# Spectral transform and experts on one core: scatters untied from the early reads, first weights converted earlier, stage 1's table filled on the chip

## The chip, the cores and the metric

One core of a Trainium2 chip runs one program. The metric is device time in microseconds (us). Of the kernel before, three runs took 837.57 to 837.99 us, with a median of 837.95.

## What is computed

The reference is a chain of three pieces in fp32:

```python
X = np.fft.fft(np.fft.fft(x, axis=1), axis=2).real      # x: (8, 3072, 256)
x = X.reshape(24576, 256)                               # tokens
logits = x @ w_gate                                     # 8 experts
# each token goes to its best expert, in order of tokens, while the
# expert has room (capacity 768); tokens without room give zero rows
h = relu(disp[e] @ w1[e]);  y = h @ w2[e]               # 256 -> 1024 -> 256
out[token] = gate * y                                   # gate: softmax value of the expert
a, b = out @ mw1, out @ mw2                             # 256 -> 1024
result = ((a * b) @ w3) @ w_out                         # -> 24576 x 256
```

The eight experts have room for 6144 tokens, so with usual inputs they are full after the first two and a half of the eight batches of 3072 tokens. All other rows of the output are zeros.

## The kernel before, in words

**Batches and stages.** Only NSTAT = 3 batches are transformed and routed, the third in a reduced form ("half"). A transform is four stages. Batch b's x comes in four chunks j (`load`, L256, 768 KB each, the last chunk of batch 0 in two cuts). `fold` (L264) lets DVE add and subtract mirrored halves into the tile xf. `stage1` (L301) multiplies xf on TensorE by the table F: 20 blocks q of 96 x 104, of which chunk j uses blocks 4j to 4j+3, and chunk 0 also the special blocks 16 to 19. In blocks 1 to 15 only 2 of the 8 columns of each group are non-zero in a given row. ACT copies the result into T (L315). `stage_d` (L322) multiplies T by the tables R into z; `stage2` (L332) multiplies z by M into A and B, ACT copies B to Bs (L353 or L355), and DVE forms rows O = A -/+ Bs (L356, L357). `packs` (L193) cuts the 13 column groups of a batch into five packs, 1 + 3 + 3 + 3 + 3.

**Tables at the start.** `tables_a(j)` (L217) loads block group j of F, and with j = 0 the special blocks and the small table S. The program at L943 puts these loads on SP's queue between the chunks of x, then G and the gate weights W (`tables_b`), R and M (`tables_c`), I and X (`tables_d`). `warm` (L956) issues matmuls on zeros; `warm(4)` stands as eight matmuls in the trace. `setup_a` (L243) multiplies G by W for the gate, `setup_b` (L250) lets DVE put the products into R.

**Routing.** `route_a` (L408) and `route_b` (L471) find each token's expert and its rank there on DVE, and from them its slot, `sloti` (L502). Slots with a large value added (`over`, L501) fall out of bounds and are not written. Then POOL issues one indirect DMA for each group of up to 128 tokens (L509): it scatters rows of O (266 floats: the transformed row, the gate, the token's number) to the rows of the DRAM tensor `disp` that the slots name. There are 24 + 24 + 13 of them. `self.scat` lists the earlier scatters, and `declare_no_dep` says that a scatter needs to wait for none of those.

**Early rows.** The first 256 rows of experts 0 to 3 (`early`, L146) are expected to be filled by batch 0 alone. `seen` (L491) keeps how many tokens batch 0 gave each expert, at most 256; if any of these four falls short, the flag at the end makes a slower second part of the program run, which redoes everything. `hand_over` (L991) gives the memory of the x tiles to the experts' class `Mlp`, asks for the first four pieces of expert weights (`raw`, L565) and for the early rows (`load_rows`, L558, the tiles X). It runs in batch 1's part of the loop, before `route_b` issues batch 1's scatters. The scatters of batch 1 and of the half batch write `disp`, which the early reads read, so they wait until these reads are done.

**Order of the work.** All engines follow program order; on SP, TensorE, DVE and ACT it is written out by hand. The loop at L1003 works pack by pack: `todo` is a list of small jobs that `fill` takes from between the packs. In the half batch (`more` is false) `halves` are two jobs that `hand_over` made: `half` (L577) converts a piece of expert 0's w1 into a high part (ACT, `split` L159) and a low part (DVE, L160), w00h/w00l and w01h/w01l. They stand behind packs 4 and 5 (`i > 2`, L1019). Then `experts` (L696) runs: first the early rows (each expert's rows are transposed, L777, split into xh and xl, multiplied by w1 into ps_h, L163 to L165, passed through relu into hh and hl, L807 and L808, multiplied by w2 into ps_y), with the half batch's routing in between, then the rest. The rest's first rows need all scatters to be done (X, L562). Conversions of other weights and the clearing of the output (L188) run at times planned in `events`. At the end `products` (L854) computes the last piece.

Of the kernel before, what the change touches and what calls it, by code (L numbers as in the profile page):

```python
# [10 lines left out]
F32 = mybir.dt.float32  # L11
# [4 lines left out]
ALU = mybir.AluOpType  # L16
# [4 lines left out]
BIG = 1048576.0  # L21


def tables():
# [32 lines left out]
    for d0, d16, sg in ((F[0], F[16], 1), (F[17], F[18], -1)):  # L57
        put(d0, 1, 2, y(32))
        put(d0, 3, 2, sg * yc(32))
        for r in (0, 1):  # L60
            put(d16, r, 4 + 2 * r, y(32 * r + 16))
            put(d16, 3 - r, 4 + 2 * r, sg * yc(32 * r + 16))
    F = F.reshape(20, 96, 104).transpose(1, 0, 2)
    S = np.zeros((24, 4, 2))
    S[:, 1, 0] = 1
    S[:, 3, 0] = -1
    S[:, :2, 1] = 1
    S[:, 2:, 1] = -1
    S = S.reshape(96, 2)
    k2 = np.arange(128)  # L70
    M = np.zeros((2, 128, 128))
    for q in range(16):
# [53 lines left out]
def body(tc, cap, x, w_gate, w1, w2, mw1, mw2, w3t, w_out, cF, cS, cM, cR, cG, cI, cH, cT, out):  # L126
# [65 lines left out]
    class Transform:  # L192
        packs = [[0], [1, 2, 3], [4, 5, 6], [7, 8, 9], [10, 11, 12]]  # L193

        def __init__(self, stack, rows_stack, p_o, p_s):
            self.p_o, self.p_s = p_o, p_s
            self.scat, self.late, self.room = [], [], None
            self.kc = kc = pool("kc", 1, stack)
            self.p_T = pool("p_T", 2, stack)
            self.p_z = pool("p_z", 3, stack)  # L200
            self.p_b = pool("p_b", 2, stack)
            self.p_x = pool("p_x", 4, rows_stack, side="right")
            self.p_f = pool("p_f", 5, rows_stack, side="right")
            p_raw = pool("p_raw", 1, rows_stack, side="right")
            self.ps1 = pool("ps1", 3, stack, space=PSUM)
            self.psd = pool("psd", 3, stack, space=PSUM)
            self.psa = pool("psa", 2, stack, space=PSUM)
            self.F = kc.tile([96, 20, 104], F32, name="F")
            self.S = kc.tile([96, 2], F32, name="S")
            self.R = kc.tile([128, 414], F32, name="R")  # L210
            self.I = p_s.tile([128, 512], F32, tag="I", name="I")[:, :352]
            self.W = kc.tile([128, 2, 8], F32, name="W")
            self.M = kc.tile([128, 2, 128], F32, name="M")
            self.X = kc.tile([128, 4, 128], F32, name="X")
            self.G = p_raw.tile([128, 2, 256], F32, tag="raw", name="G")

        def tables_a(self, j):  # L217
            if j == 0:
                nc.sync.dma_start(out=self.F[:, 16:20], in_=cF[:, 16:20])
                nc.sync.dma_start(out=self.S, in_=cS)  # L220
            nc.sync.dma_start(out=self.F[:, 4 * j : 4 * j + 4], in_=cF[:, 4 * j : 4 * j + 4])

        def tables_half(self):
            self.H = self.p_s.tile([128, 283], F32, name="H")
# [76 lines left out]
        def stage1(self, T, xf, j):  # L301
            xf, mid = xf
            F = self.F

            def part(t):
                ps = self.ps1.tile([128, 4, 104], F32, tag="ps1", name="ps")
                for i in range(4):
                    if i or j:
                        nc.tensor.matmul(ps[:, i], xf[:, t, i], F[:, 4 * j + i], start=True, stop=True)
                        continue  # L310
                    nc.tensor.matmul(ps[:, 0], xf[:, t, 0], F[:, 17 if t else 0], start=True, stop=False)
                    if t:
                        nc.tensor.matmul(ps[0:1, 0], mid, F[:, 19], start=False, stop=False)
                    nc.tensor.matmul(ps[:, 0], xf[:, t, 4], F[:, 18 if t else 16], start=False, stop=True)
                nc.scalar.copy(  # L315
                    T[:, t, :, 32 * j : 32 * j + 32].rearrange("p k (i c) -> p i k c", c=8),
                    ps.rearrange("p i (k c) -> p i k c", c=8),
                )

            return [lambda: part(0), lambda: part(1)]  # L320
# [87 lines left out]
        def route_a(self, L, where, half):  # L408
# [37 lines left out]
                nc.vector.tensor_copy(meta[:, :, 1], tid)  # L446
            first_slot = self.narrow(n, "first_slot")
            nc.vector.tensor_scalar(first_slot, m, -float(CAPP), 8.0 * CAPP - 1.0, ALU.mult, ALU.add)
            return oh, pre, tot, first_slot, where, meta

        def route_m(self, r, half):
            where, meta = r[4:]
            jobs = []
            for o, k0, n in where:
                if half:
                    for (a, b), ps, js, ks in self.halves(k0, n):
                        nc.scalar.copy(o[ps, a:b, 8 + GATE : 8 + GATE + 2], meta[ps, js])
                    jobs += [(o, j, 8, k, 128 if 0 < k < 12 else 64) for j, k in enumerate(range(k0, k0 + n))]
                else:
                    nc.scalar.copy(o[:, :, 8 + GATE : 8 + GATE + 2], meta[:, k0 : k0 + n])  # L460
                    jobs += [(o, j, 8, k0 + j, 128) for j in range(n)]
                    a, b, gs = self.mates(k0, n)
                    if a < b:
                        nc.scalar.copy(o[:, a:b, 145 + GATE : 145 + GATE + 2], meta[:, gs])
                        jobs += [(o, j, 145, 24 - k0 - j, 128) for j in range(a, b)]
            return jobs
# [4 lines left out]
        def route_b(self, r, step, half):  # L471
# [27 lines left out]
            nc.vector.tensor_add(first_slot, first_slot, rank)  # L499
            over = self.narrow(n, "over")  # L500
            nc.vector.tensor_scalar(over, rank, float(cap), BIG, ALU.is_gt, ALU.mult)  # L501
            sloti = self.p_s.tile([128, 24], I32, name="sloti", bufs=2)  # L502
            if half:
                for _, ps, js, ks in self.halves(0, 13):
# [3 lines left out]
            for o, j, c, g, w in jobs:  # L508
# [7 lines left out]
                )  # L516
                for q in self.scat:
                    tc.declare_no_dep(i.ins, q.ins, reason="every token has a row of its own")
                self.scat.append(i)
            if not half:  # L520
                nc.vector.tensor_scalar_add(tid, tid, 3072.0)
# [28 lines left out]
    class Mlp:  # L550
# [7 lines left out]
        def load_rows(self, ch):  # L558
            e, c, nt = ch
            X = self.p_X.tile([128, CT, ROW], F32, name="X")  # L560
            r0 = e * CAPP + c * 128
            nc.sync.dma_start(out=X[:, :nt], in_=disp[r0 : r0 + nt * 128].rearrange("(t p) c -> p t c", p=128))  # L562
            return X

        def raw(self, kind, e, p):  # L565
# [374 lines left out]
            k = seq.pop(0)  # L940
            xq[k] = tr.load(*k, 2 if k == (0, 3) else 1)

    for j in range(4):  # L943
        if j == 3:
            tr.tables_b()
            tr.tables_a(j)
        prefetch(1)
        if j < 3:
            tr.tables_a(j)
    tr.tables_c()  # L950
    prefetch(1)
    tr.tables_d()
# [13 lines left out]
    def go(ops):  # L966
        for op in ops:
            op()
# [8 lines left out]
    D = nc.vector  # L977
    for j in range(4):
        ops, s1 = part(0, j, T, *([D] if j < 3 else [D, D]))
        go(ops + s1)  # L980
        if j < 3:
            warm(4)
        if j == 2:
            tr.setup_a()
        prefetch(1)
    tr.setup_b()
    if HALF:
# [3 lines left out]
    def hand_over():  # L991
# [5 lines left out]
        raws = [mlp.raw(*a) for a in parts]  # L997
        for ch in early:
            rows[ch] = mlp.load_rows(ch)
        mlp.raws = dict(zip(parts[2:], raws[2:]))  # L1000
        return [lambda a=a, r=r: mlp.half(*a, r) for a, r in list(zip(parts, raws))[:2]]

    for b in range(NSTAT):  # L1003
# [8 lines left out]
        for i in range(5):  # L1012
# [3 lines left out]
                s1.append(jobs)  # L1016
            if 1 <= i < 4:
                z.append(tr.stage_d(T, tr.packs[i + 1], fill))
            if not more and i > 2:  # L1019
                todo += halves[i - 3 : i - 2]  # L1020
            where += tr.stage2(L, tr.packs[i], z[i], half, fill)
        if not more:
            break
# [43 lines left out]
    if HALF or NSTAT < NBATCH:  # L1067
        v = nc.values_load(flagi[0:1, 0:1], min_val=0, max_val=FULL)
        with tc.If(v < FULL):
            with ExitStack() as st:  # L1070
# [2 lines left out]
                p_o = pool("p_o", 8, st)  # L1073
                with ExitStack() as fs:
                    tr = Transform(fs, fs, p_o, p_s)
                    for j in range(4):
                        tr.tables_a(j)
                    tr.tables_b()
                    tr.tables_c()
                    tr.tables_d()  # L1080
# [74 lines left out]
```

## Time and profile before

| what | before |
|---|---|
| median of three runs | 837.95 us |
| the profiled execution | 836.56 us |
| its span in the profile | 834.8 us |
| TensorE (PE) busy | 802.4 us, 96% |
| DVE, ACT, POOL busy | 453.9, 370.0, 149.6 us |
| mean granted TensorE clock | 0.981 |
| DMA moved | 94.65 MB |

The profile is one execution. Its span runs from the first to the last instruction; the execution is 1.8 us longer. PE is TensorE's matmuls, PEld its weight loads. Times in the rows are us from the span's start. "idle before <-releaser" is how long the engine stood still before an instruction, and what ended that.

### The profile page before, as it was taken

The page shows a single profiled execution, that of the slowest core. Times are in us where ns is not written, and L with a number is a line of the kernel's source. Part 1 is how long each engine was busy: PE and PEld are TensorE (multiplying, and loading weights), DVE is VectorE, ACT ScalarE, POOL GpSimd, SP SyncE. Part 2 cuts the span into 40 slices and gives each one's busy share as a digit, 9 for nine tenths or more (in the row PEclk, how much of TensorE's full clock was granted, in tenths as well). Part 3 has the DMA queues.
Part 4 walks back from the last instruction along what each step waited for, and adds up shares of the span by engine and source line. Part 5 has one row for each costly group of instructions (what it writes and reads, how often), then busy time and mean ns, then how long its engine had stood idle before and what let it go on. Part 6 is the DMA issues. An engine that isn't in the chain of part 4 may idle for free.

```text
span 834.8 us, 12890 instructions
## 1 busy us (share of the span) xinstructions
PE 802.4 (96%) x5032; PEld 738.0 (88%) x5032; DVE 453.9 (54%) x874; ACT 370.0 (44%) x756; POOL 149.6 (18%) x139
## 2 busy tenths in 40 slices
PE   9999899799999999999999999999999999999992
PEld 8788799699999999999979899898898998988981
DVE  5676675498878787898542523424225234242230
ACT  2555665265545454565443433424334234243230
POOL 0047588000000000000023112121131122111101
PEclk9999899799999999999999999999999999999996
DMA  9945698476849474877100000000000000000000
GB/s 237 259 132 182 200 316 273 125 220 239 260 147 279 147 245 149 259 219 259 66 1 20 7 27 13 13 26 2 25 20 6 26 14 14 26 7 20 25 10 22
DMA packets 68822, 94.65 MB, mean 113 GB/s; under 512 B 5036, under 2 KB 56280, under 8 KB 67696
## 3 DMA queue, kind: packets, MB, share of 16 engines
q1 hardware_dynamic: 63552, 80.90, 32.0%
q0 software_dynamic: 5200, 12.84, 4.3%
q8 instruction: 41, 0.67, 0.3%
q14 instruction: 29, 0.24, 0.1%
HBM read 55.72 MB, written 39.63 MB: 114 GB/s over the span
## 4 chain that ended last, share of the span: by engine, by line
PE 80%; issue 9%; DVE 4%; DMA 3%; POOL 2%; ACT 1%; POOLq 0%; ACTq 0%; DVEq 0%; SPq 0%
PE ps_h L164 5%; PE ps_h L163 5%; PE ps_y L164 5%; PE ps_h L165 5%; PE ps_y L165 5%; PE ps_y L163 5%; PE ps_a L164 4%; PE ps_b L165 4%; PE ps_a L165 4%; PE ps_b L164 4%; PE ps_b L163 4%; PE ps_a L163 4%; PE ps_o L898 4%; PE ps_o L897 4%; PE ps_o L896 4%
## 5 line engine op out<-in xcount | busy, mean ns | idle before, releaser
L884 DVE TENSOR_TENSOR g<-ps_b,sa 128x512 f32<-128x512 f32 x96 | 66.2, 690 | 185.8 <-PE ps_b L165 179.2
L159 ACT CAST gh<-g 128x512 fp32r<-128x512 f32 x96 | 59.6, 620 | 132.9 <-DVE g L884 131.8
L160 DVE TENSOR_TENSOR gl<-g,gh 128x512 fp32r<-128x512 f32 x96 | 76.8, 800 | 65.9 <-ACT gh L159 65.9
L807 ACT ACTIVATE hh<-ps_h 128x256 fp32r<-128x256 f32 (+1 forms) x160 | 67.8, 427 | 97.3 <-PE ps_h L165 92.3
L897 PE MATMUL ps_o<-wcl,gh 128*128 128x256 f32 x384 | 108.7, 283 | 0.0
L898 PE MATMUL ps_o<-wch,gl 128*128 128x256 f32 x384 | 108.7, 283 | 0.0
L896 PE MATMUL ps_o<-wch,gh 128*128 128x256 f32 x384 | 108.6, 283 | 0.0
L160 POOL TENSOR_TENSOR yl<-yt,yh 128x512 fp32r<-128x512 f32 x24 | 30.5, 1288 | 419.5 <-ACT yh L159 419.5
L808 DVE SCALAR_TENSOR_TENSOR hl<-ps_h,hh 128x256 fp32r<-128x256 f32 (+1 forms) x160 | 74.8, 472 | 33.7 <-ACT hh L807 33.3
L509 POOL DMA_INDIRECT disp<-O,sloti x61 | 71.4, 1171 | 75.2 <-DVE acc L523 49.1
L901 POOL DMA_INDIRECT out_dram<-o,toki x48 | 47.0, 979 | 175.2 <-ACT o L900 175.2
L163 PE MATMUL ps_a<-yh,wm0h 128*128 128x512 f32 x192 | 75.0, 390 | 1.0 <-ACT yh L159 1.0
L164 PE MATMUL ps_a<-yl,wm0h 128*128 128x512 f32 x192 | 75.0, 391 | 0.7 <-POOL yl L160 0.7
L164 PE MATMUL ps_b<-yl,wm1h 128*128 128x512 f32 x192 | 74.7, 389 | 0.0
L165 PE MATMUL ps_a<-yh,wm0l 128*128 128x512 f32 x192 | 74.7, 389 | 0.0
L163 PE MATMUL ps_b<-yh,wm1h 128*128 128x512 f32 x192 | 74.7, 389 | 0.0
L165 PE MATMUL ps_b<-yh,wm1l 128*128 128x512 f32 x192 | 74.7, 389 | 0.0
L896 PEld LDWEIGHTS ps_o<-wch,gh 128*128 128x128 f32 x384 | 73.7, 192 | 0.5
L897 PEld LDWEIGHTS ps_o<-wcl,gh 128*128 128x128 f32 x384 | 73.7, 192 | 0.5
L898 PEld LDWEIGHTS ps_o<-wch,gl 128*128 128x128 f32 x384 | 73.7, 192 | 0.0
L900 ACT ACTIVATE o<-ps_o,gate 128x256 f32<-128x256 f32 x48 | 22.8, 475 | 104.7 <-PE ps_o L898 104.7
L882 ACT COPY sa<-ps_a 128x512 f32<-128x512 f32 x96 | 56.3, 587 | 11.6 <-PE ps_a L165 11.4
(179 smaller groups left out, 1952.9 us busy)
## 6 DMA issues: line engine op xcount, KB each, us to landing
out_dram<-zer SPq DMA_DIRECT2D x48, 512.0 KB, 6.5
raw<-in_w_dram SPq DMA_DIRECT2D x44, 512.0 KB, 5.2
xr<-in_x_dram SPq DMA_DIRECT2D x11, 768.0 KB, 8.4
raw<-in_w3t_dram SPq DMA_DIRECT2D x16, 512.0 KB, 4.8
raw<-in_mw_dram SPq DMA_DIRECT2D x8, 512.0 KB, 4.3
X<-disp SPq DMA_DIRECT2D x12, 266.0 KB, 4.2
X<-disp SPq DMA_DIRECT2D x8, 399.0 KB, 6.0
raw<-in_w_out_dram SPq DMA_DIRECT2D x4, 512.0 KB, 4.7
```

The lines of the kernel that those rows point to most:

```text
L159: nc.scalar.copy(hi, src)
L160: eng.tensor_sub(lo, src, hi.bitcast(F32))
L163: nc.tensor.matmul(ps, wh, ah, start=first, stop=False)
L164: nc.tensor.matmul(ps, wh, al, start=False, stop=False)
L165: nc.tensor.matmul(ps, wl, ah, start=False, stop=last)
L509: i = nc.gpsimd.indirect_dma_start(out=disp[:, :], out_offset=bass.IndirectOffsetOnAxis(ap=sloti[0:w, g : g + 1], axis=0), in_=o[0:w, j, c ...
L807: nc.scalar.activation(hi, ps, AF.Relu)
L808: nc.vector.scalar_tensor_tensor(lo, ps, 0.0, hi.bitcast(F32), ALU.max, ALU.subtract)
L884: nc.vector.tensor_mul(g, b, sa)
L896: nc.tensor.matmul(ps, hi[:, ts], Wc[0][:, f], start=f == 0, stop=False)
L897: nc.tensor.matmul(ps, hi[:, ts], Wc[1][:, f], start=False, stop=False)
L898: nc.tensor.matmul(ps, lo[:, ts], Wc[0][:, f], start=False, stop=f == 7)
```

## The change

It has three parts. First, `tr.apart` collects the early reads, and scatters are declared independent of them; so that this holds in all cases, three DVE instructions in `route_b` push the slots of later batches' tokens that would fall into the early rows out of bounds. Second, the two jobs in `halves` stand one each behind packs 2 and 3 of the half batch instead of packs 4 and 5. Third, of F only the five special blocks are loaded (F0); for blocks 1 to 15 the non-zero columns alone are loaded (D, 26 for each block, with a pattern `own` and the table S behind them), and DVE multiplies them by the pattern into F1, in four instructions of 312 or 416 columns. The loads at the start are in another order: D, the first chunk of x, F0, the other three chunks, then the other tables. `warm(4)` becomes `warm(2)`, and `setup_a` moves from behind chunk 2 to the front of chunk 3's fold and stage 1.

```diff
@@ tables()
-    F = F.reshape(20, 96, 104).transpose(1, 0, 2)
+    D = np.stack([F[1:16, :, r, :, 2 * r : 2 * r + 2] for r in range(4)], 2)
+    D = D.reshape(15, 96, 26).transpose(1, 0, 2).reshape(96, 390)
+    own = np.broadcast_to(np.repeat(np.eye(4), 2, 1), (24, 4, 8)).reshape(96, 8)
+    F = F[[0, 16, 17, 18, 19]].reshape(5, 96, 104).transpose(1, 0, 2)
...
-    S = S.reshape(96, 2)
+    S = np.concatenate([D, own, S.reshape(96, 2)], 1)
@@ class Transform
-            self.F = kc.tile([96, 20, 104], F32, name="F")
-            self.S = kc.tile([96, 2], F32, name="S")
+            self.F0 = kc.tile([96, 5, 104], F32, name="F0")
+            self.F1 = kc.tile([96, 15, 104], F32, name="F1")
+            self.F = lambda q: self.F1[:, q - 1] if 0 < q < 16 else self.F0[:, max(0, q - 15)]
+            self.D = kc.tile([96, 400], F32, name="D")
+            self.S = self.D[:, 398:400]
...
-        def tables_a(self, j):
-            if j == 0:
-                nc.sync.dma_start(out=self.F[:, 16:20], in_=cF[:, 16:20])
-                nc.sync.dma_start(out=self.S, in_=cS)
-            nc.sync.dma_start(out=self.F[:, 4 * j : 4 * j + 4], in_=cF[:, 4 * j : 4 * j + 4])
+        def tables_a(self):
+            nc.sync.dma_start(out=self.F0, in_=cF)
+
+        def spread_a(self):
+            nc.sync.dma_start(out=self.D, in_=cS)
+            own = self.D[:, 390:398].rearrange("p (r t) -> p r t", t=2).unsqueeze(1)
+            for q0, n in ((0, 3), (3, 4), (7, 4), (11, 4)):
+                D = self.D[:, 26 * q0 : 26 * (q0 + n)].rearrange("p (k t) -> p k t", t=2).unsqueeze(2)
+                shape = [96, 13 * n, 4, 2]
+                nc.vector.tensor_mul(
+                    self.F1[:, q0 : q0 + n].rearrange("p q (k r t) -> p (q k) r t", r=4, t=2),
+                    D.to_broadcast(shape),
+                    own.to_broadcast(shape),
+                )
@@ route_b
+            if early and 0 < step < NBATCH:
+                held = self.narrow(n, "sm")
+                nc.vector.tensor_scalar(held, rank, float(need), BIG, ALU.is_le, ALU.mult)
+                nc.vector.scalar_tensor_tensor(held, r[6], 8.5 - len(early), held, ALU.is_gt, ALU.mult)
+                nc.vector.tensor_add(over, over, held)
...
                 for q in self.scat:
                     tc.declare_no_dep(i.ins, q.ins, reason="every token has a row of its own")
+                for q in self.apart:
+                    tc.declare_no_dep(i.ins, q.ins, reason="later batches put nothing into these rows")
@@ load_rows
-            nc.sync.dma_start(out=X[:, :nt], in_=disp[r0 : r0 + nt * 128].rearrange("(t p) c -> p t c", p=128))
+            self.asked = nc.sync.dma_start(
+                out=X[:, :nt], in_=disp[r0 : r0 + nt * 128].rearrange("(t p) c -> p t c", p=128)
+            )
@@ body
-    for j in range(4):
-        if j == 3:
-            tr.tables_b()
-            tr.tables_a(j)
-        prefetch(1)
-        if j < 3:
-            tr.tables_a(j)
+    tr.spread_a()
+    prefetch(1)
+    tr.tables_a()
+    prefetch(3)
+    tr.tables_b()
     tr.tables_c()
...
         ops, s1 = part(0, j, T, *([D] if j < 3 else [D, D]))
+        if j == 3:
+            tr.setup_a()
         go(ops + s1)
         if j < 3:
-            warm(4)
-        if j == 2:
-            tr.setup_a()
+            warm(2)
...
         for ch in early:
             rows[ch] = mlp.load_rows(ch)
+            tr.apart.append(mlp.asked)
...
-            if not more and i > 2:
-                todo += halves[i - 3 : i - 2]
+            if not more and 0 < i < 3:
+                todo += halves[i - 1 : i]
```

## Rows read from the trace of the kernel before

**Rows 1.** The page, parts 1 and 5 (name, busy us, count, mean ns, idle).

```profile
PE 802.4 (96%) x5032; PEld 738.0 (88%) x5032; DVE 453.9 (54%) x874; ACT 370.0 (44%) x756; POOL 149.6 (18%) x139
...
L509 POOL DMA_INDIRECT disp<-O,sloti x61 | 71.4, 1171 | 75.2 <-DVE acc L523 49.1
```

**Rows 2.** The waits, all engines and SP's own: us in total, times, longest.

```profile
POOL disp L509 <- DVE O L356: 8.1, 1, 8.1
...
PE pt L777 <- DMA X<-disp: 6.3, 1, 6.3
...
PE ps_h L163 <- ACT xh L159: 2.3, 1, 2.3
...
SPq L562 <- DMA disp<-O,sloti: 20.9, 2, 11.1
```

**Rows 3.** The chain that ended last, around 150 us: start, length, what.

```profile
147.04 2.01 DMA disp<-O,sloti
149.12 2.76 DMA X<-disp
152.01 1.09 PE pt L777 x4
```

**Rows 4.** Timeline of POOL, 78 to 92 us: start, length, instruction, idle.

```profile
81.19 0.97 POOL L509 DMA_INDIRECT disp<-O,sloti  x1 [0.30 <-issue]
90.30 0.97 POOL L509 DMA_INDIRECT disp<-O,sloti  x1 [8.13 <-DVE O L356]
```

**Rows 5.** Timeline of SP: the early reads, its last transfer ahead of X.

```profile
83.67 1.91 SPq L562 DMA_DIRECT2D X<-disp  x4
...
138.66 0.55 SPq L188 DMA_DIRECT2D out_dram<-zer  x1
```

**Rows 6.** The line view of L562, 60 to 160 us, the reads of X.

```profile
DMA to landing us min/median/max: 2.8/3.2/5.7
```

**Rows 7.** Busy time by stretch: length, PE, PEld, DVE, ACT, POOL, clock, DMA, GB/s.

```profile
86.00:88.00 2.00, 2.00 (x12) 1.66 (x12) 0.94 (x2) 0.95 (x4) 0.00 (x0) 1.00 1.03 310
...
92.00:94.00 2.00, 0.58 (x1) 0.29 (x1) 2.00 (x4) 1.17 (x3) 1.70 (x2) 0.79 0.56 68
...
146.00:148.00 2.00, 0.00 (x0) 0.00 (x0) 0.00 (x0) 0.08 (x1) 1.65 (x2) 0.95 0.06 14
...
158.00:160.00 2.00, 2.00 (x20) 2.00 (x18) 1.31 (x3) 0.40 (x2) 0.00 (x0) 0.99 0.09 30
...
400.00:420.00 20.00, 18.33 (x142) 17.18 (x141) 8.08 (x21) 8.15 (x20) 2.82 (x3) 1.00 0.01 4
```

**Rows 8.** Timeline of DVE: the slots of batch 1.

```profile
77.52 0.18 DVE L507 TENSOR_TENSOR sloti<-first_slot,over 128x24 int32<-128x24 f32 x1
```

**Rows 9.** Timeline of DVE, first and last fold of batch 0.

```profile
6.47 0.17 DVE L278 TENSOR_TENSOR xf<-xr 96x6 f32<-96x6 f32 x1 [5.31 <-DMA xr<-in_x_dram]
...
18.32 0.17 DVE L278 TENSOR_TENSOR xf<-xr 96x4 f32<-96x4 f32 x1 [0.90 <-DMA xr<-in_x_dram]
...
21.05 0.41 DVE L284 TENSOR_TENSOR xf<-pr 96x254 f32<-96x254 f32 x1
```

**Rows 10.** The chain that ended last, 19 to 24 us.

```profile
19.38 1.75 PE pd L959 x8
21.12 0.79 PE pd L248 x8
21.91 1.88 PE ps L309 x16
```

**Rows 11.** Timeline of DVE, ACT and PE at the change-over to the experts.

```profile
92.30 0.57 DVE L357 TENSOR_TENSOR O<-A,Bs 128x411 f32<-128x411 f32 x1
...
92.99 0.65 ACT L159 CAST xh<-pt 128x256 fp32r<-128x256 f32 x2 [0.46 <-DVE O L357]
...
94.39 0.58 PE L164 MATMUL ps_h<-xl,w00h 128*128 128x256 f32 x1 [0.40 <-DVE xl L160]
```

**Rows 12.** Timeline of DVE: the half batch's routing begins.

```profile
98.69 0.25 DVE L414 TENSOR_REDUCE m<-L 128x13 f32<-128x104 f32 x1
```

More of the change, by code (lines that the diff above doesn't have):

```diff
@@ L196, in __init__ @@
             self.p_o, self.p_s = p_o, p_s
-            self.scat, self.late, self.room = [], [], None
+            self.scat, self.apart, self.late, self.room = [], [], [], None
             self.kc = kc = pool("kc", 1, stack)
@@ L308, in part @@
                     if i or j:
-                        nc.tensor.matmul(ps[:, i], xf[:, t, i], F[:, 4 * j + i], start=True, stop=True)
+                        nc.tensor.matmul(ps[:, i], xf[:, t, i], F(4 * j + i), start=True, stop=True)
                         continue
-                    nc.tensor.matmul(ps[:, 0], xf[:, t, 0], F[:, 17 if t else 0], start=True, stop=False)
+                    nc.tensor.matmul(ps[:, 0], xf[:, t, 0], F(17 if t else 0), start=True, stop=False)
                     if t:
-                        nc.tensor.matmul(ps[0:1, 0], mid, F[:, 19], start=False, stop=False)
-                    nc.tensor.matmul(ps[:, 0], xf[:, t, 4], F[:, 18 if t else 16], start=False, stop=True)
+                        nc.tensor.matmul(ps[0:1, 0], mid, F(19), start=False, stop=False)
+                    nc.tensor.matmul(ps[:, 0], xf[:, t, 4], F(18 if t else 16), start=False, stop=True)
                 nc.scalar.copy(
@@ L448, in route_a @@
             nc.vector.tensor_scalar(first_slot, m, -float(CAPP), 8.0 * CAPP - 1.0, ALU.mult, ALU.add)
-            return oh, pre, tot, first_slot, where, meta
+            return oh, pre, tot, first_slot, where, meta, m
         def route_m(self, r, half):
-            where, meta = r[4:]
+            where, meta = r[4:6]
             jobs = []
@@ L1075, in body @@
                     tr = Transform(fs, fs, p_o, p_s)
-                    for j in range(4):
-                        tr.tables_a(j)
+                    tr.tables_a()
+                    tr.spread_a()
                     tr.tables_b()
```

## The prediction

> **What bounds the kernel now.** I read the page first: TensorE is busy in 96% of the span, and POOL issues 61 scatters into `disp`, 1.17 us each [rows 1]. A busy share that high hides stalls, so the waits come next [rows 2]. Three are links of one chain: POOL's scatters wait once for 8.1 us, SP's loads of rows wait up to 11.1 us for scatters to land, TensorE's transposes wait 6.3 us for such a load. The chain of waits puts them in order [rows 3]: the last scatter is handed over at 147.04 and takes 2.0 us to land, SP issues X at 149.12, TensorE resumes at 152.01. So around 150 us the line of scatters sets the time, not TensorE.
>
> Where is that line late? In POOL's timeline batch 0's 24 scatters end at 82.16 and the next begins at 90.30 [rows 4]; from there 37 (24 of batch 1, 13 of the half batch) follow without a gap, the last 56.7 us behind the first. The wait bears the name of a DVE instruction of L356, but by the code a scatter of batch 1 needs something else: the four early reads of `disp` must be done, which SP issues from 83.67 [rows 5] and which land about 3 us after their issue [rows 6], the last near 89. Two more things cost TensorE time: 2.3 us at the change-over from transform to experts [rows 2], and the clock. It falls in both idle spells and is back by 158 us [rows 7]; in between the rows show 0.50. Behind 160 us every engine follows its program order behind TensorE, so what is won at 152 us should last to the end.
>
> **Part 1, the scatters.** Without the wait for the early reads, batch 1 follows batch 0 at the usual pitch of 1.28 us: at 81.19 + 1.28 = 82.47 instead of 90.30, **-7.8 us** [rows 4]. The slots must be ready by then: they are at 77.7 and three new DVE instructions add about 0.18 each, so 78.3 [rows 8], 4.2 us of cover. In the half batch the same three fall where DVE is full: 0.4 us on the early experts, used below. The run of 37 I leave at its length; its pitch of 1.58 is that of a busy DVE and DMA, and about twenty scatters change neighbours: bounds -1.5 and +1.5.
>
> The early reads now share the DMA engines with scatters. Alone they move at 310 GB/s [rows 7], 1.09 MB in 3.5 us; a scatter of 0.14 MB every 1.28 us takes 106 GB/s of that. The last read comes under 2 us later, the first some 0.4. The first lands near 86.5 and the transposes ask for it at 90.1: 3.6 us of cover, so nothing.
>
> The last scatter no longer falls into a quiet DMA. Before, SP's last transfer ahead of X was issued at 138.66 [rows 5], 8.4 us before it. Afterwards SP's come with the early experts, 3.2 us sooner (below), and the last scatter 9.1 sooner, so 2.5 us separate them. It took 2.0 us to land [rows 3]. Bounds 0 and +2, twice that; taken **+0.6**, near the row, as most of the queue has drained by then.
>
> **Part 2, the tables.** F's loads shrink from 20x104 columns to 5x104 and 400 more: 800 KB become 350. DMA paces the start: between the first chunk of x at 6.47 and the first half of the fourth at 18.32 come 2984 KB, 252 KB per us [rows 9]. Behind D the first chunk lands 0.6 us later, the second within 0.1 of before, the third 0.5 sooner (14.2), the fourth 2.7. Then DVE binds, with folds of 2.7 us and a last one of 3.1 (18.32 to 21.46): 14.2 + 2.7 + 3.1 = 20.0, -1.4. TensorE's chain is warming matmuls, gate products, stage 1 [rows 10]: stage 1 of j = 2 ends near 18.9, half the warming (0.87) and 0.79 give 20.6, then 1.88 to 22.5 instead of 23.8: **-1.3**. The gate products, now ahead of the last stage 1, need G, 3.7 MB into the queue and so there at 18.7: in time. The four filling multiplies (312 or 416 columns) take at most 0.6 each, as L357's 411 columns take 0.57 [rows 11]: 2.3 us, from D's landing near 3.5 to 6, before the first chunk at 7.1. If broadcasting doubles that, the first fold is 1.3 late, and the wait of 1.1 for the second chunk hides most of it. Bounds 0, and -1.8, the whole 450 KB. All of the transform moves with it, and the scatters too, since the slots come from there.
>
> **Part 3, the conversions.** Two, each about 1 us on ACT and on DVE, leave the change-over for packs 2 and 3; there a copy of z comes up to 0.6 us late, and TensorE, with three buffers, does not notice. In the change-over the last O of L357 ends 1.1 us sooner, which is what xh waits for, and xl no longer stands behind w01l: with part 2, xh at 90.6 instead of 92.99 and the run of matmuls at 91.45 instead of 94.39 [rows 11]. TensorE's idle spell falls from 2.3 us to 1.3, and its clock should stay up. It soon waits for the next weights, w10; the half batch's routing starts at about 95.1 instead of 98.69 [rows 12], DVE is full from there to 112, and less the 0.4 above the early experts end 3.2 us sooner: at 142.5, not 145.7. By itself this is worth **nothing**: X lands behind it.
>
> **The sum.** The transposes come at 152.0 - 1.3 - 7.8 + 0.6 = 143.5, so TensorE idles 1.0 us, not 6.3. The clock fell about 2.1 us into both idle spells (0.79 over 92 to 94, 0.95 over 146 to 148) and stayed at 1.00 over a stretch whose idle was 1.67 us in all [rows 7]. So I take it to stay at 2.4 GHz, and the 6 us from 152 to 158 then lose their 1.2 GHz: some 23 matmuls at 0.12 instead of 0.213 us, and half of the transposes' 1.09 [rows 3], **-2.5**. Altogether -1.3 - 7.8 + 0.6 - 2.5 = -11.0. The profiled execution took 836.56 us (its span 834.8 and 1.8 around it), so 825.6; it lies 1.4 below the median of the runs, 837.95, and on that scale the forecast is **827.0 us**.
>
> The Trainium skill (TensorE: Matmul & The Clock Gate, HAM oscillation) warns that a wait for DMA between bursts of matmuls sends the next burst off at the lower clock. The trace agrees after 2.3 and 6.3 us of idle, and has one stretch where 1.67 us did not do it. By that rule in its plain form the sum would be -8.5.
>
> **The rivals.**
> 1. The clock falls at the X stall after all. For it: my 1.0 us is the difference of two estimates, each uncertain by 1 us, and the spells that lowered it are only twice as long. Then the 2.5 are not won: -8.5, 829.5 us. **0.30.**
> 2. The scatters don't move, because something else holds them over the 8.1 us, as the DVE work that the wait is named after. Against it: that work hands nothing to batch 1. Only the start would be won, -1.3: 836.6 us. **0.05.**
> 3. The early reads, beside scatters, come late. The first must slip over 3.6 us before TensorE sees it, and the 1.0 us stall absorbs the next: a slip of 6 us costs some 1.4, 828.4 us. **0.07.** The Trainium skill (DMA: Bandwidth & Descriptors, Queues, rings and completion order) says that each DMA engine takes turns between queues, packet by packet. At equal turns the reads would take at most twice their time; no row shows the two together.
> 4. Slower: with eight warming matmuls cut to four, TensorE idles 1.1 us before each of two stage 1s, the clock falls near 13 us, and the thin work of stage 1 doesn't bring it back. Each us at half clock loses 0.5 on TensorE's path. A return after 6 us costs 3 (830.0); to end slower than before it must stay down for over 22 us, and 30 us give 827 + 15 = 842. Against it: behind 23 us TensorE's gaps are under 0.8. **0.03** for the slow form, 0.05 for the short one.
>
> **How the numbers follow.** The forecast has 0.50. Its own span is 824.5 (-1.8 at the start, scatters quicker) to 829; with rivals 1 and 3 the range is **824.5 to 831.0** and leaves out rival 2, the slow form of 4 and some far ends. About 0.2% (1.7 us) is what a measurement here can tell from no change: faster 0.91, same 0.05, slower 0.04.
>
> **What would show it.** No gap in POOL's scatters at 82 us and the last beginning near 138; X issued at 140 to 141, transposes near 143.5; the granted clock at 1.00 from 92 to 100 and from 146 to 158; w00h and w01h on ACT before 88; the first matmul of stage_d near 23.1 instead of 24.4. I am wrong if POOL still waits at 82 us, if the clock dips before 30, or if a new wait between 160 and 420 us eats the gain.

## The result, and the profile after

The changed kernel takes **830.85 us** in the median of four runs (827.72 to 832.36), against 837.97 (837.57 to 839.45) for the kernel before beside it: a ratio of 0.9908, 95% interval 0.9886 to 0.993. The forecast was 827.0 in a range of 824.5 to 831.0. The profiled execution took 831.45 us, its span 829.7 against 834.8. In three of the four groups of experiments below the kernel before itself took 882 to 884 us, so there only the ratio within a group counts, and a ratio takes of each kernel only the runs within 1.5% of its fastest. The two profiled executions lie 5.1 us apart where the medians lie 7.1 apart: the one before is 1.4 under its median, the one after 0.6 over.

Line numbers have moved: L509 is now L531 (scatters), L562 is L586 (loads of rows), L777 is L803 (transposes), L807 is L833 (hh), and the run of `three` is L167 to L169.

The page says little, as it did before [rows 1]: TensorE's share rose by one point.

```profile
PE 801.8 (97%) x5020; PEld 735.8 (89%) x5020; DVE 457.3 (55%) x884; ACT 369.7 (45%) x756; POOL 149.9 (18%) x139
...
L531 POOL DMA_INDIRECT disp<-O,sloti x61 | 71.7, 1176 | 65.7 <-DVE acc L547 47.5
```

The scatters' group holds the first step: 65.7 us of idle time before them instead of 75.2, at the same mean of 1.17 us. POOL's timeline shows where it went, at the place of [rows 4]:

```profile
79.81 0.98 POOL L531 DMA_INDIRECT disp<-O,sloti  x1 [0.30 <-issue]
81.09 0.97 POOL L531 DMA_INDIRECT disp<-O,sloti  x1 [0.30 <-issue]
82.37 0.97 POOL L531 DMA_INDIRECT disp<-O,sloti  x1 [0.30 <-ACT z L344]
...
136.86 1.95 POOL L531 DMA_INDIRECT disp<-O,sloti  x1 [0.30 <-issue]
```

No gap is left at 82 us: the scatter at 81.09 is the 25th, batch 1's first, 1.28 us behind the last of batch 0. From it to the last at 136.86 are 55.8 us, where it was 56.7.

The chain of waits around the X load (start, us, what) answers to [rows 3]:

```profile
136.86 5.93 DMA disp<-O,sloti
142.81 0.02 SPq L586
142.85 2.86 DMA X<-disp
146.29 0.38 ACT xh L163
```

The last scatter is handed over 10.2 us sooner, and takes 5.93 us to land instead of 2.01. SP's timeline shows what was issued behind it:

```profile
134.45 0.39 SPq L612 DMA_DIRECT2D raw<-in_w_out_dram  x1
138.05 0.37 SPq L600 DMA_DIRECT2D raw<-in_w_dram  x1
138.47 0.55 SPq L192 DMA_DIRECT2D out_dram<-zer  x1
142.85 0.88 SPq L586 DMA_DIRECT2D X<-disp  x2
```

A weight load and a clearing write, half a megabyte each, are issued 1.2 and 1.6 us after the scatter, while it is on its way. And POOL itself takes 1.95 us over it (the row at 136.86 above) instead of 0.91, beside a conversion on DVE:

```profile
136.80 1.23 DVE L164 TENSOR_TENSOR w11l<-raw,w11h 128x1024 fp32r<-128x1024 f32 x1 [1.23 <-ACT w11h L163]
```

So 1.0 of the 3.9 us is POOL's, and 2.9 lie between the end of its work and the landing. The kernel before had such landings too, ahead of its last scatter. SP issued the same two transfers there at 138.24 and 138.66; of the scatters handed over at 137.05, 139.37 and 141.92, so ahead of them, 0.7 us behind the second and 3.3 us behind it, the line view of L509 gives, one by one:

```profile
DMA to landing us min/median/max: 5.6/5.6/5.6
DMA to landing us min/median/max: 4.7/4.7/4.7
DMA to landing us min/median/max: 2.5/2.5/2.5
```

The first has the two transfers 1.2 and 1.6 us behind it and is handed over in 2.02 us, as the last scatter is now, and it landed almost as late. That it is these two alone is not shown, since older transfers are on their way as well: the DMA share is 0.89 from 137.0 to 142.7 in the profile after, and was 0.05 behind the last scatter before (147.1 to 149.0).

TensorE's own waits from 85 to 160 us (line, what it waited for, us in all, times, longest) are now small change:

```profile
PE ps_y L168 <- DVE hl L834: 1.0, 1, 1.0
PE ps_y L169 <- DVE w10l L164: 0.8, 1, 0.8
PE ps_h L168 <- DVE xl L164: 0.7, 1, 0.7
PE ps_h L167 <- ACT xh L163: 0.5, 2, 0.3
PE pt L803 <- DMA X<-disp: 0.4, 1, 0.4
```

The X load that held TensorE for 6.3 us [rows 2] holds it for 0.4; the transposes start at 145.85 instead of 152.01. The windows show the clock (us, busy time and count of PE, PEld, DVE, ACT, POOL, granted clock, DMA share, GB/s):

```profile
48.00:50.00 2.00, 1.88 (x5) 1.63 (x6) 0.23 (x2) 0.16 (x2) 1.12 (x1) 0.50 0.10 29
76.00:78.00 2.00, 2.00 (x7) 1.63 (x7) 1.80 (x8) 0.39 (x1) 1.69 (x2) 0.50 1.09 382
92.00:94.00 2.00, 1.05 (x7) 0.56 (x5) 1.57 (x4) 1.12 (x5) 1.39 (x3) 1.00 0.97 314
96.00:98.00 2.00, 1.13 (x8) 0.72 (x7) 1.63 (x3) 0.92 (x4) 1.70 (x2) 1.00 0.18 65
146.00:148.00 2.00, 1.68 (x12) 1.25 (x12) 0.90 (x4) 0.65 (x2) 0.00 (x0) 1.00 1.02 278
158.00:160.00 2.00, 2.00 (x19) 2.00 (x18) 1.85 (x4) 0.39 (x1) 0.00 (x0) 1.00 0.56 153
```

At the change-over (92 to 98) and behind X (146 to 160) the clock stays at 2.4 GHz, where it fell before [rows 7]. In this execution it drops to 1.2 GHz twice inside the transform, around 49 and 77 us, where the profile before had 1.00.

**Where the gain went.** At 164 us ACT's first three-tile xh (128x384) comes at 163.95 instead of 172.28: 8.3 us are won there, 6.2 at the wait and 2.1 by the clock. At the end 5.1 are left. The last stretch of weights takes the rest:

```profile
380.00:384.00 4.00, 4.00 (x35) 4.00 (x35) 4.00 (x10) 2.25 (x5) 0.00 (x0) 1.00 0.66 202
384.00:388.00 4.00, 2.36 (x18) 1.96 (x16) 2.61 (x6) 3.04 (x7) 0.00 (x0) 1.00 0.95 310
388.00:392.00 4.00, 3.86 (x22) 3.87 (x23) 4.00 (x8) 1.43 (x4) 0.00 (x0) 0.65 1.09 385
```

Before, the same work ran like this, 7 us later:

```profile
387.00:391.00 4.00, 4.00 (x36) 4.00 (x35) 4.00 (x11) 2.25 (x5) 0.00 (x0) 1.00 0.63 214
391.00:395.00 4.00, 3.30 (x26) 2.90 (x25) 3.68 (x8) 2.57 (x6) 0.00 (x0) 1.00 0.92 290
395.00:399.00 4.00, 3.65 (x31) 3.45 (x31) 3.40 (x8) 2.73 (x6) 0.00 (x0) 1.00 1.09 385
```

Behind the first window 40 matmuls run in 8 us instead of 57. TensorE waits for the last expert's weights (the chain of waits has the load issued at 379.06 landing 6.37 us later and its conversions behind it; the same load landed in 5.2 us before, and why it takes longer now was not found), and after 1.6 us of idle in one window the clock falls. Those 17 matmuls at 0.12 us are 2.0 us; the other 1.2 are lost in smaller steps between 164 and 380.

### The profile page after: what moved, and what is told of

It reads as the page before. It is cut to its first block, busy times and chain, and to the rows that moved or that the text cites. A ratio compares the mean times of both kernels' runs of the same rounds, so it can differ in the third digit from the quotient of the medians.

```text
span 829.7 us, 12869 instructions
## 1 busy us (share of the span) xinstructions
PE 801.8 (97%) x5020; PEld 735.8 (89%) x5020; DVE 457.3 (55%) x884; ACT 369.7 (45%) x756; POOL 149.9 (18%) x139
## 4 chain that ended last, share of the span: by engine, by line
PE 78%; issue 9%; DMA 4%; DVE 3%; POOL 2%; ACT 1%; POOLq 0%; DVEq 0%; ACTq 0%; SPq 0%
PE ps_a L168 4%; PE ps_y L168 4%; PE ps_b L169 4%; PE ps_a L169 4%; PE ps_b L168 4%; PE ps_b L167 4%; PE ps_a L167 4%; PE ps_h L168 4%; PE ps_y L169 4%; PE ps_o L924 4%; PE ps_o L923 4%; PE ps_h L167 4%; PE ps_o L922 4%; PE ps_h L169 4%; PE ps_y L167 4%
## 5 line engine op out<-in xcount | busy, mean ns | idle before, releaser
L833 ACT ACTIVATE hh<-ps_h 128x256 fp32r<-128x256 f32 (+1 forms) x160 | 67.9, 427 | 98.9 <-PE ps_h L169 92.5
L531 POOL DMA_INDIRECT disp<-O,sloti x61 | 71.7, 1176 | 65.7 <-DVE acc L547 47.5
L167 PE MATMUL ps_a<-yh,wm0h 128*128 128x512 f32 x192 | 75.0, 390 | 1.0 <-ACT yh L163 1.0
L169 PE MATMUL ps_a<-yh,wm0l 128*128 128x512 f32 x192 | 74.7, 389 | 0.0
L167 PE MATMUL ps_b<-yh,wm1h 128*128 128x512 f32 x192 | 74.7, 389 | 0.0
L169 PE MATMUL ps_b<-yh,wm1l 128*128 128x512 f32 x192 | 74.7, 389 | 0.0
```

Source lines behind the costliest of these rows:

```text
L167: nc.tensor.matmul(ps, wh, ah, start=first, stop=False)
L169: nc.tensor.matmul(ps, wl, ah, start=False, stop=last)
L531: i = nc.gpsimd.indirect_dma_start(out=disp[:, :], out_offset=bass.IndirectOffsetOnAxis(ap=sloti[0:w, g : g + 1], axis=0), in_=o[0:w, j, c ...
L833: nc.scalar.activation(hi, ps, AF.Relu)
```

## The experiments

The first question was what each part is worth alone, and which features of the profile belong to the program. A first group of four:

The changed kernel unaltered:

> The changed kernel once more, unaltered, to see which of its parts are the same in another execution. Theory A (the clock's short dips and the slow landings are part of the execution, not of the program): the last scatter again begins near 137 and the median again lies between 828 and 832, but the stretches at half clock in front of 80 us stand at other places or are missing, and with them the end of the early experts moves by 1.7 us for each. Theory B (they belong to the program): dips again at 48, 75 and 389 us, the last scatter again lands 5.9 us after its issue.

Part 1 alone, the kernel before with:

```
+            if early and 0 < step < NBATCH:
+                held = self.narrow(n, "sm")
...
+                for q in self.apart:
+                    tc.declare_no_dep(i.ins, q.ins, reason="later batches put nothing into these rows")
```

> The kernel before with the first part alone (later batches' scatters independent of the early reads). Theory: no gap in POOL's scatters at 82 us, batch 1 begins near 82.4 and the last scatter near 138.5; it lands 4 to 6 us later because SP's loads and clearing writes run beside it, so the transposes come near 147.5 instead of 152.0; the clock still falls at the change-over at 93 us. Together -4.5 for the stall and -2 for the clock behind it, less 1 to 2 given back at 160 to 400: 832 to 834 us against 838. Rival 1, the scatters' gap was all: over 9 us, as for the whole change, 829. Rival 2, something else held the scatters: 837 to 838.

Part 2 alone, the changed kernel without those lines and without those of part 3:

> The changed kernel with the first and third part taken back, so the tables' filling alone. Theory: stage_d begins 1.6 us sooner (22.8 instead of 24.4), POOL's gap of some 8 us at 80 us is there again, the transposes behind X come 1.6 sooner (near 150.4), and the end is 1.3 to 1.8 sooner, 836.2 to 836.7 us. Rival: the early start is lost at some dip of the clock in the transform before 80 us; but the scatters then still go on from the early reads, which follow from the scatters of batch 0, so 836 to 838 at most.

Part 3 alone, the kernel before with:

```
-            if not more and i > 2:
-                todo += halves[i - 3 : i - 2]
+            if not more and 0 < i < 3:
+                todo += halves[i - 1 : i]
```

> The kernel before with the third part alone (two conversions moved from the change-over to packs 2 and 3). Theory: worth nothing by itself, 837.5 to 838.5 us: the change-over is up to 1 us shorter, and the transposes behind X wait for the same scatters at 152 us, so the stall before them is longer by what the change-over gave. Rival: the change-over's stall feeds DVE's routing of the half batch and so the last scatters, which then come sooner: -1 to -2, 836 to 837.

Measured against the kernel before (883.12 us in this group): all parts **0.9876** (0.9843 to 0.9909), part 1 **1.0001** (0.9977 to 1.0024), part 2 **0.9994** (0.997 to 1.0017), part 3 **0.9899** (0.9858 to 0.994). The kernel before took 883 us here instead of 838, so no expectation in microseconds was put to the test; but the gain of part 1 did not come, part 2's small one can't be told from nothing, and part 3, expected to be worth nothing, has the only gain. Why part 3 pays here was not found. Of part 1 its trace says why. POOL's timeline:

```profile
79.60 1.02 POOL L514 DMA_INDIRECT disp<-O,sloti  x1 [0.30 <-issue]
80.92 1.09 POOL L514 DMA_INDIRECT disp<-O,sloti  x1 [0.30 <-issue]
100.55 0.97 POOL L514 DMA_INDIRECT disp<-O,sloti  x1 [18.53 <-ACT z L328]
```

and the same place in the run of part 3 alone, where the scatters still depend on the early reads:

```profile
81.20 1.02 POOL L509 DMA_INDIRECT disp<-O,sloti  x1 [0.30 <-issue]
100.24 0.97 POOL L509 DMA_INDIRECT disp<-O,sloti  x1 [18.02 <-DVE L L402]
```

With the dependency or without it batch 1 begins at 100 us, so the early reads are not what it waits for. Its slots are late, at 99.8 us instead of 77.7 [rows 8], because the transform that makes them is. DVE's timeline of part 1 alone:

```profile
99.60 0.18 DVE L512 TENSOR_TENSOR sloti<-first_slot,over 128x24 int32<-128x24 f32 x1
```

TensorE's timeline of the same run:

```profile
112.29 0.86 PE L350 MATMUL A<-z,M 128*128 128x414 f32 x2
131.28 1.75 PE L350 MATMUL B<-z,M 128*128 128x414 f32 x2 [18.13 <-issue]
```

and TensorE's and ACT's waits of that run from 55 to 140 us, two of many:

```profile
PE B L350 <- issue: 23.8, 2, 18.1
ACT z L328 <- remote: 22.1, 5, 6.8
```

Where the name is "issue" or "remote", the profile knows no cause: ACT's copies of z, whose matmuls are done, start 2 to 7 us late, TensorE once 18 us late. In this window they lie between 61 and 85 and between 112 and 131 us, beside a run of scatters; their cause was not found. What the group shows is narrower and firm: a dependency taken away is worth nothing where another input is later.

The second group asked part 1 again, the change without part 3, and two mends of what the profile after had shown.

> The kernel before with the first part alone, asked again: in its first run the kernel before took 883 us, and TensorE stood still for 18 us in front of a matmul of L350 with every input there, a stall that the traces of 838 and 831 us don't have; the scatters were not what was waited for. Theory, as before: no gap in the scatters at 82 us, the last one near 138.5, landing 4 to 6 us later, transposes near 147.5 instead of 152.0, the change-over's fall of the clock unchanged; 832 to 834 us against 838. Rival 1, the scatters' gap was all of the gain: 829 to 831. Rival 2, the early experts bind as soon as X comes sooner, since the change-over without the third part ends them near 147: 834 to 836.

The changed kernel with the two lines of part 3 put back as before:

> The changed kernel without its third part (the two conversions stay in the change-over). Theory: worth nothing alone, worth something behind the first part: the change-over keeps a stall of 2 us, the clock falls at 92 us as before, the early experts end 3 us later than without the stall, while X is there at 146: 2 to 3.5 us over the changed kernel, 833 to 834.5 us. Rival, the third part is worth nothing here either, since X binds anyway: the same as the changed kernel within 1 us, 830 to 832.

Clearing later, the changed kernel with:

```
-                    events.append(((k + 0.5) * start[-1] / len(zq), lambda: zero_out(1), None))
+                    events.append((free + (k + 0.5) * (start[-1] - free) / len(zq), lambda: zero_out(1), None))
```

> The changed kernel with the 48 writes that clear the output moved behind the early experts (from 146 us on, instead of from 98). Theory: the last scatter lands late (5.9 us instead of 2.0) because SP's weight load and clearing write are issued beside it; without the clearing writes it lands in 2.5 to 4 us, X is issued at 139.5 to 141 and TensorE's transposes are bound by the early experts alone. So at most 0.3 us are won where the clock has dipped twice before 80 us, up to 3 where it hasn't; from 146 to 400 us the writes lie closer and may cost 0 to 1 at the weights: 828.5 to 831. Rival 1, the landing is long because of the scatters in front of it on its own queue: still over 5 us, time unchanged. Rival 2, closer clearing delays the weights: over 832.

More warming:

```
+        if b:
+            spin = tr.psd.tile([128, 276], F32, name="pd")
+            warm(2)
         z = [tr.stage_d(T, pk) for pk in tr.packs[:2]]
```

> The changed kernel with two more matmuls without a reader (0.43 us each) ahead of the first stage_d of batch 1 and of the half batch, where TensorE has 8-column matmuls and a wait of 0.6 us for T behind it and the clock fell in the profile (48 and 75 us). Theory: the clock stays at 1.00 there, the copies of z come 1.7 us sooner per spared dip less some 0.3 for the matmuls, the early experts end near 142.5 to 143.5 as forecast; but X then binds at 145.8, so the end moves by 0.3 to 0.5 only: 829.5 to 831, with a smaller spread of the runs. Rival 1, the dips come at other places or don't depend on what TensorE does there: as the changed kernel, same spread. Rival 2, the matmuls cost their 1.7 us: 831 to 833.

The kernel before took 882.9 us again. Part 1 alone: 0.9989 (0.9962 to 1.0016). Without part 3: 1.0 (0.9971 to 1.0028). Clearing later: **0.9791** (0.9721 to 0.986), a ratio of three runs of 858 to 869 us. More warming: 0.992 (0.9883 to 0.9956). So of the parts only the third pays here, alone (0.9899) and by its absence. Clearing later reads lower than the changed kernel's 0.9876 (0.9843 to 0.9909), but the intervals overlap, and its six runs together have a median of 872.2 us, 0.988 of the kernel before, where the changed kernel's ten have 873.38 us, 0.989: no gain is shown. More warming shows no gain over the changed kernel's 0.9876 either. Both were meant for the state of 830 us, and neither was tried there.

The third group took the kernel before for its trace, and the clearing in another form:

> The kernel before, unaltered, for its trace where it takes 883 us instead of 838. In the traces of the eight runs so far TensorE, ACT and DVE stand for 2 to 18 us with their inputs there, and only while a run of scatters is on POOL (48 to 81 and 100 to 131 us). Theory: the same here; ACT's copies of z wait 2 to 7 us each at 61 to 84 us, so batch 1's slots come at about 100 us, some 10 us after the early reads have landed; the gap in the scatters is then not the one that the first part removes, which is why that part alone is worth nothing here. Rival: batch 1 begins at 90 to 92 us, with the early reads' landing, and the time goes elsewhere. If this run takes 838 us instead, with batch 1 at 90.3, the waits belong to where it ran and not to the kernel.

```
-                    events.append(((k + 0.5) * start[-1] / len(zq), lambda: zero_out(1), None))
+                    events.append((free + (k + 0.5) * (start[-1] - free) / 34 if k < 34 else 1e6 + k, lambda: zero_out(1), None))
```

> The changed kernel with 34 of the clearing writes spread from the end of the early experts to the end of the experts and the other 14 behind the experts, where the DMA engines are idle (share 0.00 over 400 to 420 us in the changed kernel's profile) and the first scatter into the output is still some 45 us away. Theory: as with all 48 moved behind the early experts (872 us against 883) or up to 3 us better, since the weights' loads between 160 and 400 us meet fewer of them. Rival 1: the loads there are not what TensorE waits for, so the same as that run within its spread (858 to 876). Rival 2: the last writes hold up the output's first scatters, over 880.

This time, on the same chip, the kernel before took 838 us (837.69 in the median, and 838.13 in the profiled run), so the unnamed waits don't belong to the kernel nor to that chip as such. This second trace of the kernel before is worth as much as an experiment. POOL's timeline:

```profile
82.04 0.97 POOL L509 DMA_INDIRECT disp<-O,sloti  x1 [0.30 <-issue]
92.59 0.97 POOL L509 DMA_INDIRECT disp<-O,sloti  x1 [9.58 <-ACT z L328]
```

and its windows:

```profile
50.00:52.00 2.00, 1.59 (x5) 1.35 (x6) 0.51 (x4) 0.35 (x1) 0.93 (x1) 0.50 0.69 160
77.00:79.00 2.00, 2.00 (x10) 1.75 (x10) 1.28 (x6) 0.37 (x4) 1.70 (x2) 0.55 1.08 378
98.00:100.00 2.00, 1.86 (x8) 1.87 (x9) 0.59 (x4) 0.39 (x2) 1.57 (x2) 0.50 0.89 295
152.00:154.00 2.00, 0.00 (x0) 0.00 (x0) 0.00 (x0) 0.00 (x0) 0.00 (x0) 0.57 0.68 182
```

The gap before batch 1 is there with 9.6 us. The chain that ended last runs through it here (start, us, what), and names what ended it:

```profile
82.04 3.33 DMA disp<-O,sloti
86.82 4.80 DMA X<-disp
92.59 0.39 POOL disp L509
```

Batch 0's last scatter lands, the early reads are issued, the last of them lands at 91.6, and POOL hands over batch 1's first scatter 1.0 us later. In the first trace of the kernel before the last early read landed at 89.3 and the scatter came at 90.30, again 1.0 us later. So it is the early reads that held the scatters, as the prediction had it from the code.

And the kernel before, too, can have the clock at 1.2 GHz near 50 and 78 us, which it hadn't in [rows 7]'s execution: these drops belong to the execution, as theory A of the first expectation had it.

Clearing behind took **827.96 us** (826.13 to 831.21), ratio **0.9873** (0.9844 to 0.9902): the lowest median measured, clearly under the kernel before, and 0.35% under the changed kernel's 0.9908 with overlapping intervals, so not shown to beat that. Of the 2.8 us by which its profile is shorter than the changed kernel's, some 1.6 are a drop of the clock that it lacks, the one near 76 us. Its trace bears on the long landing. SP's timeline:

```profile
136.44 0.37 SPq L600 DMA_DIRECT2D raw<-in_w_dram  x1
140.58 1.40 SPq L586 DMA_DIRECT2D X<-disp  x3
```

POOL's:

```profile
135.24 2.02 POOL L531 DMA_INDIRECT disp<-O,sloti  x1 [0.30 <-issue]
137.57 0.91 POOL L531 DMA_INDIRECT disp<-O,sloti  x1 [0.30 <-issue]
```

and TensorE's:

```profile
143.72 0.60 PE L803 MATMUL pt<-ident,X 128*128 128x128 f32 x4
```

With the weight load issued ahead of it and no clearing write behind, the last scatter lands in 2.9 us instead of 5.9; X is asked for 2.3 us sooner, and the transposes follow the early experts without a wait. The slow handover by POOL has moved to the scatter ahead, at 135.24, where DVE's w11l (135.19, 1.23 us) now falls. The other half of its expectation failed: the weights' stall near 385 us is still there (PE busy 3.44 and 4.67 of 5 us over 380 to 390, the clock at 0.66 in the second five). The writes ahead of it were only thinned, from 48 over some 290 us to 34 over some 240, so their part in it stays open.

A fourth group asked both questions on the parts once more:

> The kernel before with the first part alone, where the kernel before takes 838 us again. Theory: no gap in the scatters at 82 us, the last one near 138.5, landing 3 to 6 us later, so X's transposes near 146 to 147.5 instead of 152.0; the change-over keeps its 2 us of idle and its fall of the clock, so the early experts end at 146 to 147 too: two lines that end together. With the clock kept up behind X: -5 to -8, 830 to 833 us. Rival 1: the change-over's loss is all hidden and part one gives the whole change less the tables' 1.6, 828 to 830. Rival 2: the early experts, 3 us late, eat most of it: 834 to 836.

> The changed kernel without its third part, where the kernel before takes 838 us again. Theory: the change-over keeps TensorE idle for 2 us and the clock falls near 91 us as in the kernel before, so the early experts end 2 to 4 us later than in the changed kernel, behind X's landing at 145.8, and the time is 2 to 3 us longer than the changed kernel's: 832 to 834. Rival (the forecast's own words, worth nothing by itself): X's landing binds anyway, 830 to 831.5.

The kernel before took 884.13 us again; the ratios are 1.001 (0.9978 to 1.0041) and 0.9977 (0.9944 to 1.001). So neither expectation was put to the test at 838 us, and **what each part is worth alone there is not measured**; what follows on that rests on the two pairs of traces.

## Why the prediction was right, and where it was wrong

**The scatters (-7.8): right.** Batch 1's first scatter was put at 82.47 less the 1.3 of the start, so 81.17; it came at 81.09. The run of 37 became 0.9 us shorter, inside its bounds of 1.5. The second trace of the kernel before puts the gap at 9.6 us, so it is in the program and not in one execution; its end lies 1.0 us behind the landing of the last early read in both traces. That read as the cause was argued from the code, and these traces bear it out. The other side is shown too: where the slots come later than the reads, as at 883 us, the removal brought nothing in three runs.

**The early reads beside scatters (0): right.** The four early reads land in 3.0 to 5.0 us instead of 2.9 to 4.2, so the last of them 0.8 later, and TensorE has no wait for them before 145 us.

**The last scatter's landing (+0.6): wrong, the mis-sized term.** It rose by 3.9 us, outside its bounds of 0 and +2. The step assumed SP's queue ahead of X drained 2.5 us before the scatter, because it moved SP's loads with the early experts, 3.2 us sooner. The experts hardly moved, the scatter did, and it fell into a busy DMA, with two transfers of SP's issued just behind it: 2.9 of the 3.9 lie there. The other 1.0 is POOL's handover beside DVE's conversion, which the step didn't look for at all. For the place that it assumed, 2.5 us behind SP's transfers, the +0.6 was well chosen, as a scatter 3.3 us behind them landed in 2.5 us in the kernel before; it was the place that was wrong, and the same trace had a landing of 5.6 us for the place that came. In the last variant, without the clearing write and with the conversion one scatter earlier, it took 2.9 us. The Trainium skill (DMA: Bandwidth & Descriptors, Latency and other measured facts) puts an access to HBM at 0.2 us on average and 2 us at high load. The traces agree in direction: the same scatter needs 2.0 us in a quiet DMA, in both traces of the kernel before, and 5.9 in a busy one; no run here tells the access to HBM apart from the queue in front of it.

**The start (-1.3): right.** The first stage_d matmul came at 22.76 instead of 24.38, so -1.6, between its bounds. The four filling multiplies took 1.99 us in all, 2.98 to 4.97, where 2.3 were allowed for.

**The change-over and the early experts (-3.2): wrong in this pair of executions.** They ended at 145.5, only 0.2 sooner. The step left out the clock inside the transform. Two drops to 1.2 GHz, each costing about 1.7 us, ate the 1.6 of the start and as much again; so xh came at 92.50 instead of 90.6. With one drop instead of two, in the last variant, the transposes behind them come at 143.7. The forecast's 142.5 is thus, by an estimate from these two, what no drop would give, within 0.5. The second trace of the kernel before has drops at the same two places and ends its early experts at 149.4; against that one they end 3.9 sooner. So the gain of the start and the change-over is there, and what the clock did in one execution hid it.

**The idle of 1.0 us and the clock that stays up (-2.5): right in effect, by luck in its reason.** TensorE idled 0.4 us before X. But not because X came at 143.5: X let TensorE go on at 145.85, 2.4 us later than that, and the early experts were late by 3.0. The clock stayed at 1.00 and brought 2.1. (The step's own terms, 23 matmuls by 0.093 us and half of 1.09, add to 2.7 and not to 2.5.) Rival 1, the clock falling at the X stall after all, did not happen. The Trainium skill's rule on waits for DMA between bursts (TensorE: Matmul & The Clock Gate, HAM oscillation) and the traces agree where the wait was long (6.3 us before, and 5.0 in the second trace of the kernel before, with 0.57 at 152 to 154).

**The sum.** In the two profiles of before and after 8.3 of the 11.0 were won by 164 us; against the second trace of the kernel before it is 10.1 (163.95 instead of 174.10). Then came what the prediction named as its danger, a new wait between 160 and 420 us: 3.2 us lost, 2.0 of them in front of the last expert's weights and in the drop of the clock behind that stall. The sentence that failed is that what is won at 152 us should last to the end. That leaves 5.1, which is 5.9 short; in the medians, the scale of the forecast, 7.1 were won, so 827.0 was 3.9 too fast. The range held 830.85 by its upper end, which reached there for rivals 1 and 3 and not for this: that the time lies inside is in part luck.

## What to carry to other kernels

A gap in a line of transfers is worth its length only where the dependency removed is the last input: compare it with the second-latest one, here the slots, which were in time at 838 us and 18 us behind batch 0's last scatter at 883. When a chain is pulled forward, list again what every other queue issues beside its end; a transfer that something waits for lands later among bulk transfers (5.9 us here, 2.9 with the clearing writes out of the way), though moving them was not shown to shorten the whole. And a gain in the middle of a kernel that is bound by several things is not a gain at its end: look for the next wait, with its margin, behind it.

## What was not expected of the hardware

- The clock can drop to 1.2 GHz without a wait of TensorE to speak of: at 76 to 78 us of the profile after with TensorE busy 2.00 of 2.00 us there and in the windows of 2 us from 72 on, and near 50 and 78 in the second trace of the kernel before, while the first has 1.00 through the same work. What decides it is open.
- An indirect scatter's landing went from 2.0 us in a quiet DMA to 5.9 in a busy one, with two half-megabyte transfers issued just behind it, and back to 2.9 with one issued just ahead. Its handover on POOL often grows, from 0.91 to as much as 2.0 us, beside a conversion of two SBUF inputs on DVE; not always, as the scatter at 88.77 of the profile after takes 0.97 us beside w01l.
- On one chip the kernel before took 838 us in one group of runs and 883 in two others, and on a second chip 884; at 883 and 884 us the traces have waits of 2 to 23 us that no row explains, beside runs of scatters.
